# Block-sparse attention and Fourier mixing: gate queries regrouped by key block, the causal bound moved from bias matmuls into the maxima

## The chip, the core and the metric

The kernel runs on one core of a Trainium2 chip. The metric is device time in microseconds of one execution, as the median of several runs. Lower is better. A separate profiled execution gives the profile; its span is the time from the first to the last instruction.

## The reference

There are two stages. The first is attention over 4 batches of 8 heads, 768 positions and 64 features per head. Keys are cut into 12 blocks of 64. A query sees its own block and the three blocks whose mean key scores highest among the blocks that aren't in its future:

```python
k_rep = k.reshape(B, H, n_blocks, block, D).mean(axis=3)
gate_scores = np.einsum('bhsd,bhnd->bhsn', q, k_rep)
gate_scores = np.where(causal, gate_scores, -1000000000.0)
top_idx = np.argsort(gate_scores, axis=-1)[..., -top_k:]
# mask: the chosen blocks and the query's own block, and pos_q >= pos_k
attn = softmax(where(mask, q @ k.T / sqrt(D), -1e9)) @ v
```

The second takes x, the attention output as 4 x 768 x 512, and mixes it with a two-dimensional Fourier transform and a feed-forward layer:

```python
mixed = np.real(np.fft.fft(np.fft.fft(x, axis=1), axis=2))
u = x + mixed
un = (u - mean(u)) / sqrt(var(u) + 1e-6)
out = u + maximum(un @ w_ch1, 0) @ w_ch2        # 512 -> 2048 -> 512
```

## The kernel before

**Units of work.** Two heads of one batch make a pair P, 0 to 15; four pairs make a batch b. For a pair the kernel loads q and k (Lq, Lk: two DMAs each, 192 KB a DMA, three buffers each) and v (Lv, one DMA, two buffers). TensorE transposes both (tq, tk, L306, six 128x128 fp32 blocks each). From the transposed k, DVE sums each block of keys (ks, L311) and spreads the sums for both heads (kh); ACT casts k to fp16 (kc). DVE keeps q in fp32 (qc, L330), GpSimd casts it (qs, through the helper `pcopy` at L242).

**The gate.** g_mm (g) multiplies the fp32 queries by the block sums. Its output has the blocks of one head on 32 partitions and queries along the free axis, in four groups of 32 partitions. For pairs 0 to 6 (P < NX) groups 0 and 1 hold the two halves of the queries from 128 on for one head, groups 2 and 3 those of the other; for pairs 7 to 15 each group holds 192 consecutive queries and both heads. Four more fp16 matmuls (L351, L360) with the tables czl and czr (czl2, czr2) add a huge negative number wherever a block lies in the query's future. g_turn (gt, L366) transposes 32x32 blocks, so that a partition is a query; g_max (gx, L373) takes the eight largest of the 12 values for each query and head, in 10 or 12 instructions; g_less (gl, two steps) marks the blocks that lie below the third largest and multiplies the marks by a table oth (oth2), which is 0 for the query's own block and -60000 elsewhere; g_back (gm, L396) transposes back into the tile mt.

**How the mask reaches the scores.** For pairs 0 to 6 the score tile (s:P,i, L416) gets more matmuls (L427), which add mt for the keys' blocks; SC_MASK lists them. For pairs 7 to 15, stage_K (K, L401) copies mt into rows 64 to 95 of the fp16 q tile, and the scores are one matmul of 96 rows (L421). ACT takes the exponential (e, L436), GpSimd clears the upper triangle of diagonal blocks (d, L442), TensorE multiplies by v (v, L454), DVE divides (x, L465). vc is GpSimd's cast of v.

**The second stage.** fs and fd fold x on DVE, f (f:b,0 to 3, L498 to L508) folds again; y and m are the two Fourier matmuls (L523, L557, L558) with ty (ACT) and tr (DVE, L543) between them; u adds x (L571), xu rescales on ACT, xt and un turn the result into the layout of the feed-forward layer. w:b,it (L633, L635) are the 16 steps of the first feed-forward matmul, r their relu, c (L652) the second matmul, o (L658) the last addition and od the store. bn, nv, nr make the variance. pg:b is a small GpSimd copy that waits for f.

**Weights.** W:0, W:1 (load_w1) and X:0, X:1 (load_w2) are DMAs issued by GpSimd; they cast fp32 to fp16 on the way, 1024 KB each as written. All q, k, v loads and stores are issued by SP. LT brings the Fourier tables, Lc and Li smaller constants.

**The order.** Nothing is scheduled at run time. The text ORDER (L130) is a list of steps such as `g:7` or `s:7,5`, and every engine executes its share of them strictly in this order, with waits on its data and buffers. So moving a step in ORDER moves it in the queue of every engine that it uses. All PSUM tiles come from one pool of four buffers in turn.

Of the kernel before, what the change touches and what calls it, by code (L numbers as in the profile page):

```python
# [19 lines left out]
S = 768  # L20
# [8 lines left out]
def _consts_np():  # L29
# [22 lines left out]
    g, i = p // 32, p % 32  # L52
    b = np.arange(10)
    qq = Q0 + 320 * (g % 2)[:, None] + 32 * b[None, :] + i[:, None]
    oth = np.where((qq // 64)[:, :, None] != nn, NEG, 0.0)

    czl = np.zeros((NB, 32), np.float32)
    czl[:, 0:NB] = np.where(nn[None, :] > nn[:, None], NEG, 0.0)
    czr = 16384.0 * (s[None, Q0:] // 64 == nn[:, None])
# [6 lines left out]
    qq = 192 * (p // 32)[:, None] + 32 * np.arange(6)[None, :] + (p % 32)[:, None]  # L66
    oth2 = np.zeros((128, 6, 2, 16), np.float32)
    oth2[:, :, :, 0:NB] = np.where((qq // 64)[:, :, None, None] != nn, NEG, 0.0)
    czl2 = np.zeros((3, 4, 2, 16), np.float32)
    for gg in range(4):  # L70
        for j in range(3):
            czl2[j, gg, :, 0:NB] = np.where(nn > 3 * gg + j, NEG, 0.0)
    czr2 = 16384.0 * (np.arange(192)[None, :] // 64 == np.arange(3)[:, None])
    ind = np.zeros((2, 32, S), np.float32)
    for e in range(2):
# [7 lines left out]
                czl=czl.astype(np.float16), czr=czr.astype(np.float16),  # L83
                indc=indc.reshape(128, 24).astype(np.float16),
                oth2=oth2.reshape(128, 192).astype(np.float16),
                czl2=czl2.reshape(3, 128).astype(np.float16), czr2=czr2.astype(np.float16),
                ind=ind.transpose(1, 0, 2).copy().astype(np.float16),
                half=half.reshape(128, 24))

# [16 lines left out]
for _pieces in SC_TILES:  # L106
    SC_OFF.append(_w)
    _n = sum(_q1 - _q0 for (_, _q0, _q1) in _pieces)
    _m = []
    _o = 0  # L110
    for (_jt, _q0, _q1) in _pieces:
        for _q in range(_q0, _q1, 128):
            for _e in range(2):
                COL[_e, _jt, _q // 128] = _w + _e * _n + _o + _q - _q0
        for _h in range(2):
            _c0 = Q0 + 320 * _h
            _a = max(_q0, _c0, 192, 128 * _jt + 64)
            _b = min(_q1, _c0 + 320)
            if _a < _b:
                _m.append((_jt, _h, _o + _a - _q0, _a - _c0, _b - _a))  # L120
        _o += _q1 - _q0
    SC_MASK.append(_m)
    _w += 2 * _n
# [7 lines left out]
Lq:1 Lk:1 Lq:2 Lk:2 tk:0 tq:0 ks:0 Lq:3 Lk:3 qc:0 tq:1 iz:1 kh:0 qs:0 g:0 Lq:4 Lv:0 Lv:1 qc:1 iz:0  # L131
kc:0 tk:1 gt:0 gx:0 kc:1 gl:0,0 tq:2 gl:0,1 gm:0 Lq:5 Lk:4 ks:1 s:0,2 s:0,3 qc:2 e:0,2 tk:2 kh:1
e:0,3 Lk:5 g:1 d:0,2 ks:2 qs:1 s:0,4 gt:1 kc:2 qs:2 s:0,0 gx:1 e:0,4 s:0,5 tq:3 kh:2 gl:1,0 e:0,5
Lq:6 s:0,1 qc:3 tk:3 e:0,1 gl:1,1 qs:3 gm:1 g:2 e:0,0 ks:3 d:0,5 tq:4 d:0,4 gt:2 d:0,0 kc:3 s:1,2
kh:3 d:0,1 qc:4 s:1,1 d:0,3 e:1,2 s:1,0 vc:0 gx:2 s:1,3 e:1,1 g:3 Lv:2 Lq:7 gl:2,0 gl:2,1 e:1,3
d:1,1 gm:2 v:0 gt:3 e:1,0 d:1,3 gx:3 s:1,5 s:2,5 x:0 s:2,0 e:1,5 e:2,5 d:1,5 s:2,1 e:2,0 d:2,5
tq:5 gl:3,0 d:1,0 e:2,1 Lq:8 Lk:6 vc:1 s:1,4 qc:5 s:2,4 e:1,4 fs:0,0 s:2,3 Lv:3 fs:0,1 tk:4 gl:3,1
e:2,3 d:1,4 gm:3 tk:5 d:1,2 ks:4 e:2,4 d:2,0 v:1 d:2,1 ks:5 qs:4 kc:4 kh:4 d:2,3 x:1 s:2,2 vc:2
g:4 Lc:0 e:2,2 d:2,4 Lv:4 Lk:7 Lk:8 LT:0 kh:5 qs:5 s:3,2 gt:4 kc:5 s:3,5 gx:4 s:3,0 e:3,5 s:3,1
e:3,2 gl:4,0 tq:6 gl:4,1 e:3,0 d:3,2 gm:4 g:5 d:3,5 qc:6 e:3,1 d:2,2 s:3,4 d:3,0 gt:5 s:4,3 e:3,4  # L140
fs:1,0 s:3,3 gx:5 tq:7 e:3,3 fs:1,1 v:2 gl:5,0 qc:7 d:3,3 d:3,4 gl:5,1 tk:6 vc:3 x:2 e:4,3 s:4,4
d:3,1 Lv:5 ks:6 s:4,0 vc:4 e:4,4 v:3 gm:5 Lv:6 Lq:9 Lk:9 Lq:10 e:4,0 fs:2,1 kh:6 fs:2,0 s:5,5 x:3
kc:6 d:4,0 s:5,1 e:5,5 s:5,0 e:5,1 fd:2,0 s:4,1 fs:3,0 s:5,2 e:5,0 fs:3,1 fd:2,1 g:6 fd:3,0 e:4,1
fd:3,1 s:4,2 gt:6 e:5,2 s:5,4 f:0,3 s:5,3 e:4,2 f:0,2 tk:8 f:0,1 e:5,4 y:0,1 f:0,0 e:5,3 ks:8
d:5,4 d:4,2 y:0,0 tr:0,1 d:5,3 kc:8 W:0 gx:6 d:4,1 s:4,5 d:5,1 ty:0,1 tr:0,0 tk:7 d:5,0 pg:0 d:4,3
e:4,5 ks:7 ty:0,0 m:0,2 W:1 gl:6,0 kc:7 d:5,2 m:0,1 u:0,2 d:5,5 vc:5 m:0,0 u:0,1 xu:0,2 d:4,4 Lv:7
Lk:10 v:5 qs:6 u:0,0 qs:7 xu:0,1 xt:0,2 tq:8 xu:0,0 un:0,2 d:4,5 xt:0,1 kh:8 qc:8 xt:0,0 kh:7
gl:6,1 v:4 qs:8 un:0,1 un:0,0 gm:6 g:7 vc:6 x:5 w:0,1 Lv:8 Lq:11 gt:7 x:4 w:0,3 r:0,1 gx:7 s:6,5
s:6,4 e:6,5 fs:4,1 s:6,2 gl:7,0 e:6,4 w:0,0 fs:5,1 gl:7,1 fs:4,0 e:6,2 gm:7 d:6,4 r:0,3 tq:9 K:7
r:0,0 g:8 Lq:12 Lk:11 qc:9 s:6,1 gt:8 s:6,3 e:6,1 bn:0,3 d:6,2 s:6,0 d:6,5 w:0,7 vc:7 gx:8 e:6,0  # L150
qs:9 e:6,3 tk:9 r:0,7 w:0,8 Lk:12 Lv:9 ks:9 fs:5,0 s:7,5 gl:8,0 r:0,8 w:0,11 kh:9 gl:8,1 kc:9 gm:8
K:8 w:0,2 r:0,11 e:7,5 bn:0,0 s:7,4 r:0,2 g:9 bn:0,1 d:6,3 e:7,4 s:7,0 d:6,0 d:6,1 tq:10 gt:9
e:7,0 bn:0,4 vc:8 s:7,3 qc:10 s:7,1 e:7,3 d:7,0 tk:10 d:7,5 gx:9 d:7,4 e:7,1 s:7,2 Lk:13 Li:0
Lq:13 Lv:10 ks:10 tq:11 e:7,2 d:7,1 w:0,12 gl:9,0 kh:10 kc:10 bn:0,5 d:7,2 X:0 w:0,15 qc:11 r:0,12
gl:9,1 X:1 v:6 r:0,15 bn:0,2 d:7,3 s:8,4 qs:10 gm:9 g:10 e:8,4 x:6 v:7 K:9 gt:10 s:8,5 x:7 s:8,3
e:8,5 w:0,5 e:8,3 gx:10 w:0,10 d:8,3 r:0,5 fs:6,0 fs:6,1 gl:10,0 s:8,2 gl:10,1 r:0,10 fs:7,1
w:0,14 fd:6,1 e:8,2 fs:7,0 fd:6,0 s:8,0 fd:7,1 r:0,14 s:9,5 fd:7,0 w:0,13 e:8,0 f:1,1 f:1,0 e:9,5
s:8,1 r:0,13 s:9,1 qs:11 tk:11 e:8,1 w:0,9 ks:11 e:9,1 vc:9 kc:11 s:9,2 f:1,3 Lv:11 Lk:14 y:1,0
d:8,5 f:1,2 r:0,9 d:8,2 e:9,2 pg:1 s:9,4 vc:10 tr:1,0 tq:12 e:9,4 d:8,4 Lv:12 Lq:14 gm:10 y:1,1
d:8,0 kh:11 ty:1,0 qc:12 d:9,4 vc:11 w:0,6 nv:0 ty:1,1 d:9,2 Lv:13 d:8,1 g:11 tr:1,1 K:10 r:0,6  # L160
tq:13 gt:11 m:1,0 qc:13 s:9,3 u:1,0 s:9,0 e:9,3 w:0,4 gx:11 e:9,0 m:1,1 bn:1,1 r:0,4 d:9,0 d:9,1
s:10,4 xu:1,0 u:1,1 d:9,3 v:8 d:9,5 gl:11,0 un:1,0 s:10,5 gl:11,1 e:10,4 v:9 vc:12 gm:11 bn:1,0
e:10,5 K:11 Lv:14 Lq:15 xu:1,1 x:8 s:10,2 c:0,0,0 e:10,2 un:1,1 fs:8,1 d:10,4 fs:8,0 s:10,3 d:10,2
x:9 s:10,1 vc:13 e:10,3 c:0,1,0 Lv:15 e:10,1 fs:9,1 d:10,3 bn:1,2 nr:0 s:11,5 bn:1,3 s:11,2 e:11,5
s:10,0 s:11,4 e:10,0 c:0,1,1 e:11,4 d:10,1 e:11,2 tk:12 d:11,5 tk:13 Lk:15 ks:12 d:11,2 d:11,4
s:11,3 kh:12 c:0,0,1 ks:13 e:11,3 kh:13 kc:12 d:11,3 qs:13 c:0,4,0 o:0,1 kc:13 od:0,1 o:0,0 d:10,0
# [614 lines left out]
```

## Time and profile before

| | us |
|---|---|
| median of 3 runs | 306.3 |
| lowest and highest | 306.24, 306.63 |
| profiled execution | 307.28 |
| its span | 305.2 |

The costliest groups, as one line each of the page: second feed-forward matmul (L652) 86.0 us busy on TensorE, first one (L633 and L635) 84.7 and 69.7, exponentials (L436) 83.0 on ACT, the diagonal selects (L442) 38.5 on GpSimd.

A row of a group reads: line, engine, operation, output<-input by the program's names, the shape, the count; after the first bar the busy time and the mean duration of one in nanoseconds; after the second bar the engine's idle time just before them and what ended it. DVE, ACT and GpSimd durations can overlap a little in a group, so that busy time by count is nearer to the step from one to the next. Matmuls are pipelined: their durations hold a latency of the pipeline, and the distance from start to start says what a matmul takes of the stream. A timeline's row has start, length, engine, line and, in brackets, idle time before it with its releaser. Rows of a table by stage have the stretch and its length, and then busy time (with the number of instructions) of PE, PEld, DVE, ACT and POOL, TensorE's granted clock, DMA share and GB/s.

### The profile page before, as it was taken

Reading aid. Unit: us, or ns where it says so; the run is one execution under the profiler, and the core shown is the slowest. Engines: PE = TensorE matmul, PEld = TensorE weight load, DVE = VectorE, ACT = ScalarE, POOL = GpSimd, SP = SyncE. Lnnn points to the kernel's source line nnn. Section 1 sums busy time; section 2 is a strip of 40 time slices with the busy share of each in tenths; the row PEclk is TensorE's granted clock in tenths of the full one; section 3 lists DMA queues with packets and bytes.
Section 4 is the critical chain, followed back from the end, with each engine's and each line's share of the span. In section 5 each row is a group of like instructions: output and inputs, shape, how many; then the busy total and the mean of one; then the engine's idle time right before and its main releaser. Section 6 shows DMA issues by size and latency. Waiting matters only on the chain.

```text
span 305.2 us, 6705 instructions
## 1 busy us (share of the span) xinstructions
PE 291.8 (96%) x2638; PEld 179.2 (59%) x2638; DVE 194.4 (64%) x581; ACT 163.2 (53%) x205; POOL 106.5 (35%) x247
## 2 busy tenths in 40 slices
PE   7789996999999999999999999999999999999994
PEld 3557674766676674675577665655666545565441
DVE  1888998999997998699689720773671217700013
ACT  1579989747968967846663779004266001056000
POOL 2165726837682687763470443000030000200000
PEclk9999999999999999999999999999999999999999
DMA  9999989999999998610110001112200011100013
GB/s 172 211 213 206 210 183 274 191 219 193 218 181 194 213 177 163 165 38 34 38 69 2 2 1 34 37 69 71 103 3 0 0 71 69 69 2 0 0 71 137
DMA packets 89467, 32.83 MB, mean 108 GB/s; under 512 B 82704, under 2 KB 85084, under 8 KB 89436
## 3 DMA queue, kind: packets, MB, share of 16 engines
q1 hardware_dynamic: 84108, 27.69, 41.5%
q0 software_dynamic: 3136, 4.19, 8.1%
q10 hardware_dynamic: 2192, 0.52, 0.9%
q8 instruction: 21, 0.34, 0.5%
q14 instruction: 10, 0.08, 0.1%
HBM read 28.73 MB, written 6.29 MB: 115 GB/s over the span
## 4 chain that ended last, share of the span: by engine, by line
PE 80%; DVE 12%; DMA 4%; ACT 2%; SPq 1%; issue 1%; DVEq 0%
PE c L652 27%; PE h L633 18%; PE h L635 9%; PE sc L421 6%; PE av L454 5%; PE tp L306 4%; DMA nat<-in_q_dram 4%; PE yp L523 3%; DVE u L571 2%; PE sc L416 2%; ACT pt L436 1%; PE g L357 1%; PE sc L427 1%; PE mx L557 1%; PE mx L558 1%; DVE tr L543 1%
## 5 line engine op out<-in xcount | busy, mean ns | idle before, releaser
L436 ACT ACTIVATE pt<-sc 128x1024 f16<-128x1024 f32 (+1 forms) x96 | 83.0, 924 | 22.1 <-PE sc L421 15.2
L652 PE MATMUL c<-w_sb,hT 128*128 128x512 f16 x384 | 86.0, 379 | 0.0
L633 PE MATMUL h<-unT,w 128*128 128x512 f16 x256 | 84.7, 379 | 0.0
L635 PE MATMUL h<-unT,w 128*128 128x256 f16 x256 | 69.7, 272 | 0.0
L652 PEld LDWEIGHTS <-hT 128*128 128x128 f16 x384 | 37.3, 98 | 42.7
L645 ACT ACTIVATE hT<-h 128x768 f16<-128x768 f32 x48 | 37.9, 814 | 41.7 <-PE h L635 41.6
L442 POOL TENSOR_SCALAR_AFFINE_SELECT pt<-pt 128x256 f16<-128x256 f16 x96 | 38.5, 422 | 42.3 <-ACT pt L436 41.3
L658 DVE SCALAR_TENSOR_TENSOR u<-c,rs,u 128x512 f32<-128x512 f32 x24 | 17.2, 744 | 46.2 <-PE c L652 46.2
L633 PEld LDWEIGHTS <-w 128*128 128x128 f16 x256 | 25.0, 98 | 28.9 <-issue 0.4
L306 PE MATMUL tp<-id,nat 128*128 128x128 f32 x192 | 26.7, 277 | 3.2 <-DMA nat<-in_q_dram 1.8
L583 ACT ACTIVATE x<-u,nm 128x512 f16<-128x512 f32 x24 | 15.9, 720 | 23.1 <-DVE nm L577 23.0
L242 POOL TENSOR_SCALAR_AFFINE_SELECT qk<-q 64x768 f16<-64x768 f32 (+1 forms) x25 | 20.6, 827 | 18.7 <-DVE q L330 13.1
L635 PEld LDWEIGHTS <-w 128*128 128x128 f16 x256 | 25.0, 98 | 3.5
L421 PE MATMUL sc<-qk 96*128 96x512 f16 (+3 forms) x144 | 26.6, 305 | 0.1
L306 PEld LDWEIGHTS tp<-id,nat 128*128 128x128 f32 x192 | 21.2, 141 | 8.0 <-issue 2.2
L239 POOL TENSOR_TENSOR t<-vr,rs 128x6 f32<-128x6 f32 x12 | 2.5, 207 | 60.5 <-DVE rs L614 59.8
L454 PEld LDWEIGHTS <-pt 128*128 128x128 f16 x672 | 22.1, 97 | 2.3 <-issue 1.0
L454 PE MATMUL av<-v,pt 128*128 128x65 f16 x672 | 23.0, 193 | 0.2
L242 POOL TENSOR_SCALAR_AFFINE_SELECT qk<-mt 32x384 f16<-32x384 f16 x36 | 18.6, 518 | 10.0 <-DVE mt L396 8.4
L643 DVE TENSOR_SCALAR hT<-h 128x768 f16<-128x768 f32 x16 | 15.0, 945 | 10.3 <-PE h L635 10.3
L571 DVE SCALAR_TENSOR_TENSOR u<-mx,x 128x512 f32<-128x512 f32 x24 | 15.5, 684 | 8.7 <-DMA out_dram<-u 4.4
L537 ACT CAST ty<-yp 128x772 f16<-128x772 f32 x8 | 8.0, 1045 | 19.2 <-PE yp L523 18.0
(84 smaller groups left out, 357.9 us busy)
## 6 DMA issues: line engine op xcount, KB each, us to landing
nat<-in_v_dram SPq DMA_DIRECT2D x16, 384.0 KB, 6.0
out_dram<-u SPq DMA_DIRECT2D x24, 256.0 KB, 2.0
nat<-in_k_dram SPq DMA_DIRECT2D x31, 192.0 KB, 4.5
nat<-in_q_dram SPq DMA_DIRECT2D x31, 192.0 KB, 5.1
w<-in_moe_w_ch_dram POOLq DMA_DIRECT2D x2, 1024.0 KB, 11.2
w_sb<-in_moe_w_ch_dram POOLq DMA_DIRECT2D x2, 1024.0 KB, 14.1
fs_sb<-c_FS SPq DMA_DIRECT2D x1, 582.0 KB
fd_sb<-c_FD SPq DMA_DIRECT2D x1, 384.0 KB, 6.4
```

Of the source, the lines that this page charges most:

```text
L242: nc.gpsimd.affine_select(out=out, in_=in_, pattern=[[0, i] for i in n], base=0, channel_multiplier=0, compare_op=ALU.is_ge, fill=0.0)
L306: nc.tensor.transpose(ps[:, 128 * st:128 * st + 128], src[:, st, :], id32)
L421: nc.tensor.matmul(ps[:, e, co:co + q1 - q0], qk[0:96, e, 1, 128 * jt:128 * jt + 128], qk[0:96, e, 0, q0:q1], start=True, stop=True)
L436: nc.scalar.activation(out=d["pt"][:, o:o + 2 * n].rearrange("p (e c) -> p e c", e=2), in_=d["sc", i][:, :, 0:n], func=AF.Exp, scale=0.125)
L442: nc.gpsimd.affine_select(out=dg, in_=dg, pattern=[[0, 2], [1, 128]], base=0, channel_multiplier=-1, compare_op=ALU.is_ge, fill=0.0)
L454: nc.tensor.matmul(av[:, e, 66 * st:66 * st + 65], pt[:, co:co + 128], vv[:, e, jt, 0:65], start=(cnt == 0), stop=(cnt == 20))
L571: nc.vector.scalar_tensor_tensor(out=u_b[:, k2, :].rearrange("p (m two) -> p two m", two=2), in0=mps[:, k2, :].rearrange("p (two m) -> p t ...
L633: nc.tensor.matmul(hp[:, 0:512], w1s, unT[:, dt, 0:512], start=(dt == 0), stop=(dt == NDT - 1))
L635: nc.tensor.matmul(hp[:, 512:768], w1s, unT[:, dt, 512:768], start=(dt == 0), stop=(dt == NDT - 1))
L645: nc.scalar.activation(out=hT, in_=hp, func=AF.Relu)
L652: nc.tensor.matmul(c_ps[b, g[0]][:, st - g[0], :], h_t[b, it][:, 128 * st:128 * (st + 1)], w2_sb[:, it, :], start=(it == 0), stop=(it == N ...
L658: nc.vector.scalar_tensor_tensor(out=o, in0=c_ps[b, g[0]][:, st - g[0], :], scalar=st_t[b][1][:, st:st + 1], in1=o, op0=ALU.mult, op1=ALU.add)
```

## The change

Queries of a gate are regrouped, so that all rows of a column block have the same own key block. For pairs 0 to 6 a group takes every other run of 32 queries; for pairs 7 to 15 every fourth run. Blocks of 64 queries thus lie side by side in different groups, and the number of blocks that a query may see depends, nearly everywhere, on the column block alone. g_max can then take its maximum over just the allowed blocks (at least eight values), and no bias matmul is needed. Where fewer than eight blocks are allowed, the values beyond the bound are overwritten: by a minimum with a table lim for pairs 0 to 6, by three memsets for pairs 7 to 15. Column blocks whose queries see three or fewer blocks are left out. The table oth is now the same for all rows. The mask's matmuls and stage_K's copies follow the new grouping: each is split in two.

The core of the diff (tables of constants, and the tiles' declarations, cut):

```diff
 def g_mm(P):            # pairs 0 to 6
+            qq = d["q32"][:, Q0:S].rearrange("p (b w i) -> p b w i", w=2, i=32)
             for c in range(4):
-                c0 = Q0 + 320 * (c % 2)
-                nc.tensor.matmul(g[32 * c:32 * c + 32, :], kr_s[slot][:, c // 2, :],
-                                 d["q32"][:, c0:c0 + 320], start=True, stop=False)
-            for c in range(4):
-                c0 = 320 * (c % 2)
-                nc.tensor.matmul(g[32 * c:32 * c + 32, :], czl, czr[:, c0:c0 + 320],
-                                 start=False, stop=True)
+                nc.tensor.matmul(g[32 * c:32 * c + 32, :].rearrange("p (b i) -> p b i", i=32),
+                                 kr_s[slot][:, c // 2, :], qq[:, :, c % 2, :], start=True, stop=True)
...
 def g_turn(P):
+        if P < NX:
+            d["gt"] = gt = apool.tile([128, 320], FP, tag="gt", name=f"gt_{P}", bufs=1)
+            nc.vector.transpose(out=gt, in_=d["g"])
+            x = gt.rearrange("p (b n) -> p b n", n=32)[:, 1:5, 4:8]
+            tt(x, x, lim, ALU.min)
+            return
...
+        nc.vector.memset(gt[0:64, 35:205].rearrange("p (b c) -> p b c", c=34)[:, :, 0:17:16], -3e38)
+        nc.vector.memset(x[:, 1, :, 4:6], -3e38)
+        nc.vector.memset(x[:, 1:3, :, 6:8], -3e38)
 def g_max(P):
-        for j in range(nj):
-            nc.vector.max(out=mx[:, j, :], in_=d["gt"][:, w * j:w * j + NB])
+        for j in range(1 if P < NX else 2, nj):
+            n = max(8, j + 3 if P < NX else j // 2 * 2 + 2)
+            nc.vector.max(out=mx[:, j, :], in_=d["gt"][:, w * j:w * j + n])
 def g_less(P, j):       # pairs 7 to 15: ten column blocks of 12 in place of 12 of 16
-            tt(d["lt"], d["lt"], oth2, ALU.mult)
+                tt(l, l, oth2.rearrange("p b e n -> p (b e) n")[:, 2:12, 0:NB], ALU.mult)
...
 def stage_K(P):
         for c in range(4):
-            pcopy(qk_s[P % NSLOT][64:96, :, 0, 192 * c:192 * c + 192],
-                  mt[32 * c:32 * c + 32, :].rearrange("p (o x) -> p o x", o=1)
-                  .to_broadcast([32, 2, 192]), [2, 192])
+            for e in range(2):
+                pcopy(qk_s[P % NSLOT][64:96, e, 0, :]
+                      .rearrange("p (b w i) -> p b w i", w=4, i=32)[:, :, c, :],
+                      mt[32 * c:32 * c + 32, :].rearrange("p (b i) -> p b i", i=32), [6, 32])
 def s_mm(P, i):         # pairs 0 to 6: the mask
-        for jt, w, o, a, wid in (SC_MASK[i] if P < NX else []):
-            for e in range(2):
-                nc.tensor.matmul(ps[:, e, o:o + wid], indz[w][hs[e], 128 * jt:128 * jt + 128],
-                                 mt[hs[e], a:a + wid], start=False, stop=True,
-                                 skip_group_check=True)
+        for jt, o0, o1, a in (SC_MASK[i] if P < NX else []):
+            for w in range(2):
+                for e in range(2):
+                    nc.tensor.matmul(ps[:, e, o0:o1].rearrange("p (b w i) -> p b w i", w=2, i=32)
+                                     [:, :, w, :], indz[w][hs[e], 128 * jt:128 * jt + 128],
+                                     mt[hs[e], a:a + (o1 - o0) // 2].rearrange("p (b i) -> p b i", i=32),
+                                     start=False, stop=True, skip_group_check=True)
```

The memsets and loads of the four bias tables go; a load of lim (8 KB) and a memset of the now permanent tile ltb come.

ORDER is written anew from the first step to the last. It holds the same steps, each once. Two excerpts show its manner; first the loads and the beginning, then the surroundings of the first feed-forward step `w:0,1`:

```diff
-Lq:1 Lk:1 Lq:2 Lk:2 tk:0 tq:0 ks:0 Lq:3 Lk:3 qc:0 tq:1 iz:1 kh:0 qs:0 g:0 Lq:4 Lv:0 Lv:1 qc:1 iz:0
+Lk:1 Lk:2 Lq:1 Lq:2 tk:0 tq:0 ks:0 Lq:3 Lk:3 qc:0 tk:1 iz:1 kh:0 qs:0 g:0 ks:1 iz:0 gt:0 kc:0 tk:2
...
-gl:6,1 v:4 qs:8 un:0,1 un:0,0 gm:6 g:7 vc:6 x:5 w:0,1 Lv:8 Lq:11 gt:7 x:4 w:0,3 r:0,1 gx:7 s:6,5
+vc:5 kc:8 ks:7 v:4 d:5,5 u:0,1 W:1 xu:0,0 m:0,2 d:5,2 d:5,3 ks:8 X:0 s:6,3 xu:0,1 u:0,2 v:5 e:6,3
+kh:7 x:4 s:6,5 xu:0,2 d:6,3 s:6,2 qs:7 x:5 xt:0,1 e:6,5 e:6,2 s:6,1 un:0,1 xt:0,2 d:6,5 e:6,1 qs:8
+xt:0,0 un:0,2 g:7 un:0,0 s:6,0 s:6,4 gt:7 e:6,0 d:6,1 tq:9 fs:5,1 Li:0 Lv:7 gx:7 e:6,4 w:0,1 Lq:12
+d:6,0 kh:8 bn:0,4 d:6,4 tk:9 gl:7,0 r:0,1 gl:7,1 w:0,7 gm:7 kc:9 qc:9 K:7 w:0,0 r:0,7 ks:9 w:0,2
```

Further steps that stand elsewhere in it: before, W:0 stood behind tr:0,1, d:5,3 and kc:8 and ahead of pg:0; now it stands behind pg:0, vc:4, d:4,2 and d:4,3. Before, X:0 and X:1 stood near pair 7's and 8's scores; now X:0 follows W:1 and X:1 stands near pair 8's scores. y:0,0 now stands between f:0,0 and f:0,3. Before, Lq:9 and Lk:9 stood behind Lv:6; now Lq:9, Lk:8, Lv:5, Lq:10 and Lk:9 stand ahead of Lv:6.

## The prediction

> **What bounds the kernel now.** I read the page's busy shares and slices first, then the same by stage, then the chain of waits in order of time, then the groups kept apart by shape, then DMA and timelines of single stretches.
>
> ```profile
> PE 291.8 (96%) x2638; PEld 179.2 (59%) x2638; DVE 194.4 (64%) x581; ACT 163.2 (53%) x205; POOL 106.5 (35%) x247
> ...
> 0.00:9.00 9.00, 6.60 (x25) 3.16 (x26) 2.20 (x7) 1.49 (x2) 1.90 (x18) 1.00 0.92 172
> 9.00:41.00 32.00, 29.25 (x434) 20.18 (x434) 28.77 (x111) 26.42 (x33) 16.23 (x32) 1.00 1.09 205
> 41.00:66.00 25.00, 21.07 (x319) 15.39 (x318) 23.35 (x63) 19.70 (x25) 14.29 (x25) 1.00 1.09 223
> 66.00:118.00 52.00, 51.87 (x551) 35.24 (x548) 47.71 (x158) 40.95 (x52) 33.28 (x62) 1.00 1.06 195
> 118.00:301.00 183.00, 183.00 (x1318) 105.28 (x1316) 91.61 (x244) 74.67 (x95) 40.77 (x112) 1.00 0.16 45
> ```
>
> Columns: stretch, length, busy PE, PEld, DVE, ACT, POOL, granted clock, DMA share, GB/s. From 66 us, the first step w of the feed-forward, TensorE never stands still: what leaves its stream there comes off the end. Before 66 us DVE is the fullest (28.8 of 32, 23.4 of 25), DMA is full too. Busy PE flatters: a 512-column c matmul takes 1.73 / 8 = 0.216 us of stream (chain), 0.42 ns a column. Starts against columns leave PE gaps of 7.5 us from 9 to 41, about 8.2 from 41 to 66, 3.5 from 66 to 118 (2.0 in gaps over 60 ns), 5.3 after.
>
> ```profile
> 49.80 1.02 DVE L239 TENSOR_TENSOR fg<-zw 128x762 f16<-128x762 f16 x2
> ...
> 53.23 1.02 DVE L543 CAST tr<-yp 128x768 f16<-128x768 f32 x1 [1.26 <-PE yp L523]
> 54.14 0.80 DVE L373 MAX8 mx<-gt 128x8 f32<-128x12 f32 x10
> 55.15 1.03 DVE L543 CAST tr<-yp 128x768 f16<-128x768 f32 x1 [0.20 <-PE yp L523]
> ```
>
> So even in batch 0's Fourier stage DVE waits only 1.5 us for y.
>
> ```profile
> L373 DVE MAX8 mx<-gt 128x8 f32<-128x12 f32 x178 | 14.3, 155 | 0.2
> L242 POOL TENSOR_SCALAR_AFFINE_SELECT qk<-mt 32x384 f16<-32x384 f16 x36 | 18.6, 518 | 10.0 <-DVE mt L396 8.4
> L360 PE MATMUL g<-czr,czl 128*32 128x192 f16 x36 | 2.4, 246 | 0.0
> L351 PE MATMUL g<-czr,czl 128*32 128x320 f16 x28 | 2.2, 299 | 0.0
> ...
> 71.73 0.53 PE L357 MATMUL g<-q,krb 128*32 128x192 f32 x8
> 72.08 0.27 PE L360 MATMUL g<-czr,czl 128*32 128x192 f16 x4
> 72.28 0.39 PE L416 MATMUL sc<-qk 64*128 64x256 f16 x4
> ```
>
> The four bias matmuls of a gate run side by side in four column groups: one pass, not four. Last view, DMA from 54 to 64 us, while the casting load of w1 runs on POOL's queue q0 and all q, k, v loads stand on q1:
>
> ```profile
> q0 software_dynamic: 881, 1.77, 96.0%
> q1 hardware_dynamic: 711, 0.18, 13.0%
> ```
>
> **What the Trainium skill says.** "TensorEngine Tiling (Array Packing)", Key Properties: changing the tiling mode drains TensorE. The trace agrees: from the first bias matmul to the score matmul behind it 0.20 us pass, 0.08 of them columns. That drain stays. "PSUM — Partial Sum Buffer", Specifications: non-contiguous access patterns slow matmuls significantly; no matmul of before writes PSUM with gaps, so this trace can't say. "DMA: Bandwidth & Descriptors", Issuing engines are not separate DMA queues: SP's and POOL's transfers share 16 engines and interleave. The trace shows how unevenly: 1.77 MB against 0.18.
>
> **The change, part by part.** The profiled execution took 307.28 us, 305.2 of span and 2.1 around it; the runs' median is 306.3. I sum differences and put them on 306.3.
>
> *Bias matmuls gone.* 7 gates lose 320 columns (0.135 us each, 0.95), 9 lose 192 (0.081, 0.73). The nine lie in or near the full stretch: -0.7. The seven lie where PE has gaps: worth 0 to -0.9; I take 0. The gate's query is now read in runs of 32 fp32 at a stride: no row; 0 to +0.3 us a gate (its fp32 passes doubled, 0.32); I take 0, since runs are long.
>
> *Mask matmuls (pairs 0 to 6).* 11 two-head couples become 16 of half width; columns stay 2176 a head and pair (0.91 us of stream, both heads side by side). The 64-wide ones were already issued 29 ns apart, so only the two 32-wide ones cost more than columns: 7 x 0.03 = 0.2 us in the stage with gaps, 0. Gapped PSUM writes: below, as a rival.
>
> *DVE.* Pairs 0 to 6: one MAX less (14.3 / 178 = 0.08), one small tensor_tensor more (the 128x24 one takes 0.17 to 0.21; I take 0.17), shorter compares -0.03: +0.06 x 7 = +0.4. Pairs 7 to 15: two MAX less (-0.16), 72 elements less in compare and product (-0.13), three memsets more (the 128x6 one takes 0.063): -0.1 x 9. Near zero; the limit of extent saves at most 4 ns a MAX.
>
> *POOL.* stage_K goes from 4 copies of 384 elements to 8 of 192. From 422 ns at 256, 518 at 384 and 826 at 768 elements a 192 one costs about 0.374: 3.0 us in place of 2.07, +8.3 over nine pairs. POOL is busy 35%, so only latency counts. For pair 7 the new order has two w and one gate between gm and the first score (2 x 1.28 + 0.47 = 3.0 us of PE), where before 5.6 us stood: 0 to 1.5 (if a copy stays at 0.5); I take +0.5.
>
> *Constants.* Four small tables go, one (8 KB) comes; ACT's queue issues one DMA less and SP two less. All behind the first loads: 0.
>
> *The order.* ORDER is rewritten throughout with the same steps, so each engine's queue moves. I compared which steps stand ahead of three points. Ahead of the first w: newly all six score tiles of pair 6 and tq:9 (PE +2.7 us), x:4, fs:5,1, gt:7, gx:7 (DVE +2.7 net of kh:8). DVE sets that point, so w starts 2.7 + 0.4 later; y:0,0 is now begun while f:0,3 and f:0,2 still run on DVE, and qc:8 and gl fill its wait, which takes back up to 1.5 us of waiting: w starts 1.6 later, with 2.7 of PE work less behind it: -1.1. From there to the first c: c:0,0,0 comes ahead of 7.8 us of DVE and 5.3 of PE steps, so PE gets filler that needs no DVE; of the 2.0 us in larger gaps (0 to -2.0) I take -0.6. After 118 us nothing is to be had: the last tail (c, o, od) has the same form.
>
> *SP and POOL queues.* SP brings the q and k loads in another order. To the start of W:0's packets (53.4 us) q1 had moved 11.1 MB, in written order up to Lv:6. X:0 stood near 86 us; now W:0, W:1 and X:0 follow one another on POOL. At 6.4 us each (1.77 MB in 10 us, 1.05 MB each; X nearer 7) they take the engines for about 20 us, not 13. W:0 itself comes later: f ends about 1 us later, and pg:0, vc:4 and two selects (0.18 + 0.90 + 2 x 0.42) stand ahead: packets from about 56.2, with 11.1 + 2.8 x 0.21 = 11.7 MB moved. The load that PE wants first behind this is Lk:9, complete at 11.9 MB, wanted by tk:9 near 69 us (behind the first w). The missing 0.2 MB come at 18 KB/us x 13 us = 0.23 MB: just in time. I take 0.
>
> Sum: -0.7 - 1.1 - 0.6 + 0.5 = -1.9: 304.4 us.
>
> **Rivals.**
> *A, the forecast:* 304.4, own range 302.8 to 305.6.
> *B, only what is certain:* the new order's gains are paid back by small stalls of its own; then the bias passes' 0.7 less the wait for K: 306.1. For: each order is laid by estimates. Against: PE has filler ahead of each DVE group.
> *C, slower: the third weight load starves Lk:9.* If under about 11.65 MB are moved when W:0's packets begin, the trickle doesn't finish it, and tk:9, which stands in PE's queue ahead of w:0,7, waits to near 75.5 us. Price up to 6.5 us: 304.4 + 6 = 310; a late half costs 2 to 3. For: the margin above is a few hundred kB. Against: q1 stood below its rate from 40 to 45 us before (slices 183 after 210) and may gain.
> *D, slower: gapped PSUM writes.* If the mask matmuls take twice their columns, 7 x 0.91 = 6.4 us come into the stage with 15.7 us of PE gaps; about half hidden, 304.4 + 3.2 = 307.6. Twice is an estimate from the page's "significantly"; runs of 32 columns speak for less, a gain is excluded.
>
> **How the numbers follow.** A 0.45, better than A's range 0.03, B 0.13, C 0.23, D 0.12, other stalls of the order 0.04. A difference under 0.2% (0.6 us) can't be told from none here. Faster 0.48, same 0.13 (B), slower 0.39. The range 302.6 to 309.0 leaves out the best 0.03 and the worse half of C, and takes in D and the unknown strides; A's own stands above.
>
> **What would show it.** Right: no bias group; a gate followed by its successor after 0.47 us; first w near 67.5 us with pair 6's scores ahead; PE gaps from 66 to 118 under 3 us; PE full after. K copies near 0.37 us. Wrong: a gap ahead of tk:9 ended by a k load (C); L427's 128-wide and 64-wide starts further apart than their columns (D); gate starts further apart than 0.16 us; first pair-7 score late by more than 1.5 us on POOL's copies.

## The result and the profile after

| | before | after |
|---|---|---|
| median, us | 306.27 | 315.40 |
| lowest and highest | 306.12, 306.63 | 313.85, 316.50 |
| profiled execution, its span | 307.28, 305.2 | 315.76, 313.8 |

The change makes the kernel slower: 1.0293 of the time before, 95% interval 1.0247 to 1.0339. Forecast were 304.4 us, range 302.6 to 309.0. (Of some versions below, single executions take several us longer than the others: the medians count them, the ratios leave the longest out.)

The page of after, its slices (each digit tenths of a slice of 7.8 us; PEclk is the granted clock) and the chain of waits:

```profile
PE   7798999873999999999999999999999999998995
...
PEclk9999999996899999999999999999999999999999
...
PE 80%; DMA 10%; DVE 4%; SPq 3%; issue 1%; ACT 0%; POOL 0%; DVEq 0%
```

Two slices of PE, from 63 to 78 us, fall to 7 and 3 tenths, and from 71 to 86 us the granted clock falls as well. Nothing else in the row stands out. So the loss sits in one place. TensorE's waits of after, the longest first (total, times, longest):

```profile
PE tp L291 <- DMA nat<-in_k_dram: 8.6, 3, 7.4
...
PE c L648 <- ACT hT L641: 0.9, 1, 0.9
...
PE tp L291 <- DVE u L567: 0.8, 1, 0.8
```

In before's list of TensorE's waits no load of k stands at all. The place, in TensorE's timeline of after:

```profile
68.08 0.38 PE L629 MATMUL h<-unT,w 128*128 128x512 f16 x1
68.30 0.27 PE L631 MATMUL h<-unT,w 128*128 128x256 f16 x1
75.95 1.51 PE L291 MATMUL tp<-id,nat 128*128 128x128 f32 x6 [7.38 <-DMA nat<-in_k_dram]
77.26 0.63 PE L629 MATMUL h<-unT,w 128*128 128x512 f16 x1
77.68 0.42 PE L631 MATMUL h<-unT,w 128*128 128x256 f16 x1
...
80.40 0.38 PE L629 MATMUL h<-unT,w 128*128 128x512 f16 x1
80.62 0.27 PE L631 MATMUL h<-unT,w 128*128 128x256 f16 x1
```

w:0,1 ends, and tk:9 waits for Lk:9. Then everything takes longer until 80.4 us: from one L629 to the next L631 0.42 us pass instead of 0.22. The table by stage says why. Its columns are those of the prediction's first view; the number after POOL's is the granted clock:

```profile
66.00:68.40 2.40, 2.40 (x22) 1.49 (x16) 2.30 (x19) 1.94 (x2) 1.39 (x4) 1.00 1.15 198
68.40:73.50 5.10, 0.17 (x2) 0.00 (x0) 1.78 (x5) 0.81 (x1) 3.86 (x11) 1.00 1.22 197
73.50:80.30 6.80, 4.35 (x16) 2.65 (x17) 0.24 (x1) 1.59 (x2) 1.05 (x2) 0.50 1.05 218
```

TensorE stands from 68.4 us; at 73.5 its clock is halved, for 6.83 us in the records, to 80.33. From 75.95 on TensorE works 4.4 us at half clock and loses 2.2.

I laid the whole difference out over TensorE's stream: the starts of its instructions against the columns that they have (0.42 ns each; these sums depend a little on how matmuls that run side by side are counted, by up to 0.2 us a row). Before ends at 300.88 us = 271.38 of columns + 29.50 of gaps; after at 309.76 = 269.68 + 40.08. Half speed counts as gap here.

| us | before | after | difference |
|---|---|---|---|
| columns | 271.38 | 269.68 | -1.70 |
| gaps 0 to 66 | 20.73 | 20.04 | -0.69 |
| 66 to 80 | 0.82 | 9.67 | +8.85 |
| 80 to 118 | 2.68 | 2.50 | -0.18 |
| 118 to 145 | 1.13 | 2.15 | +1.02 |
| 145 to 200 | 2.25 | 2.51 | +0.26 |
| from 200 | 1.89 | 3.21 | +1.32 |

So 8.85 us come from the stall and the half clock behind it, and two small new gaps add 1.0 (ahead of tk:13, which waits for a PSUM tile that u:1,2 reads) and 1.07 (in the last tail). Up to 118 us there are gains as forecast, -1.70, -0.69 and -0.18; which of them shorten the kernel is taken up at the end.

Last, the transfers of after from 55 to 75 us, with the casting weight loads on q0 and the q, k, v loads on q1 (packets, MB, share of 16 engines):

```profile
q0 software_dynamic: 2089, 3.14, 87.3%
q1 hardware_dynamic: 3714, 0.93, 28.1%
```

Three weight loads, 3.14 MB, go through in 20 us, while the q, k and v loads get 0.93 MB. Lk:9's halves were issued at 54.24 and 55.99 us and landed at 73.35 and 75.81.

### The profile page after: what moved, and what is told of

The parts are those of the page before. It is cut to its first block, busy times and chain, and to the rows that moved or that the text cites. A ratio compares the mean times of both kernels' runs of the same rounds, so it can differ in the third digit from the quotient of the medians.

```text
span 313.8 us, 6743 instructions
## 1 busy us (share of the span) xinstructions
PE 292.7 (93%) x2644; PEld 179.1 (57%) x2644; DVE 193.5 (62%) x591; ACT 163.6 (52%) x205; POOL 110.9 (35%) x279
## 4 chain that ended last, share of the span: by engine, by line
PE 80%; DMA 10%; DVE 4%; SPq 3%; issue 1%; ACT 0%; POOL 0%; DVEq 0%
PE c L648 27%; PE h L629 18%; PE h L631 9%; DMA nat<-in_k_dram 8%; PE sc L415 7%; PE av L450 6%; PE tp L291 5%; PE yp L519 3%; SPq L274 2%; DMA nat<-in_v_dram 2%; PE mx L553 1%; PE mx L554 1%; PE g L341 1%; PE sc L410 1%; PE yp L525 1%
## 5 line engine op out<-in xcount | busy, mean ns | idle before, releaser
L629 PE MATMUL h<-unT,w 128*128 128x512 f16 x256 | 86.2, 384 | 0.0
L631 PE MATMUL h<-unT,w 128*128 128x256 f16 x256 | 70.4, 275 | 0.0
L438 POOL TENSOR_SCALAR_AFFINE_SELECT pt<-pt 128x256 f16<-128x256 f16 x96 | 37.6, 411 | 50.0 <-ACT pt L432 49.1
L629 PEld LDWEIGHTS <-w 128*128 128x128 f16 x256 | 25.3, 99 | 29.2 <-issue 1.7
L291 PE MATMUL tp<-id,nat 128*128 128x128 f32 x192 | 27.6, 282 | 11.4 <-DMA nat<-in_k_dram 8.6
L229 POOL TENSOR_SCALAR_AFFINE_SELECT qk<-mt 32x192 f16<-32x192 f16 x72 | 25.4, 373 | 10.1 <-DVE mt L389 8.5
L631 PEld LDWEIGHTS <-w 128*128 128x128 f16 x256 | 25.3, 99 | 4.0
L226 POOL TENSOR_TENSOR t<-vr,rs 128x6 f32<-128x6 f32 x12 | 2.4, 198 | 56.8 <-DVE rs L610 56.2
L310 ACT CAST qk<-tp 64x768 f16<-64x768 f32 x18 | 14.3, 792 | 8.5 <-PE tp L291 8.4
```

Of the source, the lines that this page charges most:

```text
L229: nc.gpsimd.affine_select(out=out, in_=in_, pattern=[[0, i] for i in n], base=0, channel_multiplier=0, compare_op=ALU.is_ge, fill=0.0)
L291: nc.tensor.transpose(ps[:, 128 * st:128 * st + 128], src[:, st, :], id32)
L438: nc.gpsimd.affine_select(out=dg, in_=dg, pattern=[[0, 2], [1, 128]], base=0, channel_multiplier=-1, compare_op=ALU.is_ge, fill=0.0)
L629: nc.tensor.matmul(hp[:, 0:512], w1s, unT[:, dt, 0:512], start=(dt == 0), stop=(dt == NDT - 1))
L631: nc.tensor.matmul(hp[:, 512:768], w1s, unT[:, dt, 512:768], start=(dt == 0), stop=(dt == NDT - 1))
```

## The experiments

Theory T: Lk:9 is caught behind three weight loads in a row on POOL's queue, which get nearly all of the DMA engines; the stall and the half clock after it are the loss. Rivals: R1, the new gate itself costs time; R2, the new order loses in other places. The first four runs shared one chip; before there was 306.81 us (305.59 to 308.65).

### X:0 moved away

```diff
- ... d:5,3 ks:8 X:0 s:6,3 xu:0,1 ...        + ... d:5,3 ks:8 s:6,3 xu:0,1 ...
- ... Lk:11 d:7,3 K:8 g:9                    + ... Lk:11 d:7,3 K:8 X:0 g:9
```

> The changed kernel with one step moved: X:0 (the third weight load) from behind W:1 to behind K:8. Theory T (the q and k loads stand still while three weight loads run one behind the other; tk:9 waits for Lk:9, and TensorE then runs at half clock for a while): the stall of 7.5 us and the 2.2 us lost at half clock go, 315.4 - 9.7 = 305.7, between 304.7 and 307. Rival R1 (the new gate itself costs: more GpSimd copies, gapped PSUM writes, more small DVE work): stays at 312 or more. Rival R2 (the rewritten order loses in many places): 309 to 313.

Measured: median 309.95 us (307.06 to 315.85), ratio 1.0083 (1.0041 to 1.0124). Two of the seven executions took 307.1 and 307.3, four 309.5 to 310.9; the profiled one was the longest, 315.85. In its trace the stall behind the first w is gone, but another load was caught, Lk:8's second half, issued 1.4 us before W:0 (in after 4.0 us before it):

```profile
62.89 1.51 PE L291 MATMUL tp<-id,nat 128*128 128x128 f32 x6 [4.55 <-DMA nat<-in_k_dram]
```

The expected 304.7 to 307 was missed by all seven, by 0.3 us or less in the two shortest. X:0 does make the loss larger: the median fell by 5.4 us. In the profiled execution the load that was caught had been issued 2.9 us later than in after, and when W:0's packets began 10.59 MB had moved, in place of 11.26 in after. What the four of 309.5 to 310.9 lost, no trace shows.

### Lk:9 ahead of Lq:10

```diff
- ... d:3,1 Lv:5 Lq:10 Lk:9                  + ... d:3,1 Lv:5 Lk:9 Lq:10
```

> The changed kernel with two neighbouring loads exchanged: Lk:9 is issued ahead of Lq:10; the three weight loads stay together. T: Lk:9 needs 11.5 MB moved in place of 11.9, lacks about 0.25 MB when the weight loads begin and comes with the trickle near 62 to 64 us, ahead of its use at 68.4; Lq:10 comes near 75.8 and is wanted near 78. So 305.5 to 307.5. If the weight block as such harms (POOL, HBM traffic), not the order of the loads: 312 or more. R1: 312 or more.

Measured: 306.39 us (305.73 to 311.76), ratio 0.9991 (0.9974 to 1.0009). Two tokens exchanged bring back 9 us, with all three weight loads where they were. Gaps from 66 to 80 us are 0.78 us; TensorE's waits on k loads fall from 8.6 to the first line below (its list of waits), and the clock row of the page has no dip:

```profile
PE tp L291 <- DMA nat<-in_k_dram: 1.0, 2, 0.6
```

```profile
PEclk9999999999999999999999999999999999999999
```

T holds: the caught load is the loss. The margin is small: Lk:9's second half landed at 66.85 us, about 1.5 us ahead of its use.

### The new gate in the old order, and the old gate in the new order

The first takes all functions of after and ORDER of before, the second the reverse.

> The new gate with the order of the kernel before. T: the gate is no cost; TensorE loses 1.7 us of stream, of which 0.7 in the full stretch: 305.0 to 306.5. R1: most of the 9 us appears, 311 or more. In between (307 to 310) would say that the longer copies of stage_K cost where the old order leaves little room.

Measured: 306.78 us (305.54 to 309.03), ratio 1.0002 (0.9980 to 1.0024). R1 falls. Nor does the gate gain anything that could be measured: columns fall by about 1.6 us, but gaps grow by 0.89 before 66 us and by 0.32 from 80 to 118.

> The kernel before with the new order: old gate with bias matmuls. T: the same wait ahead of tk:9 and the same half clock, 315 to 318 (1 us above the changed kernel at most, for the bias matmuls). R1: near 306 to 309.

Measured: 316.85 us (315.37 to 318.64), ratio 1.0335 (1.0292 to 1.0378). The old gate in the new order shows the same picture, with a longer wait at the same transposes and the same 6.83 us of half clock. Its tk:9, in TensorE's timeline:

```profile
77.11 1.51 PE L306 MATMUL tp<-id,nat 128*128 128x128 f32 x6 [8.30 <-DMA nat<-in_k_dram]
```

The order alone carries the loss, and the run with Lk:9 first says which two of its steps. So R2 falls as well, but for the two small gaps.

### The stall filled with idle work

```diff
 def a_tp(P, who):
+        for _ in range(32 if (P, who) == (9, 1) else 0):
+            nc.tensor.matmul(ps[:, 0:512], id16, fs_sb.rearrange("p a b c k -> p (a b c k)")[:, 0:512],
+                             start=True, stop=True)
```

> The kernel after, and ahead of tk:9's six transposes 32 matmuls of 512 columns that nobody reads, into the same PSUM tile (32 x 0.213 = 6.8 us, so from 68.4 to 75.2 us of the stall's 75.9). Theory T (the half clock behind the stall is the answer to an idle TensorE and a cost of its own, 4.4 us at half = 2.2 us): the load still lands at about 75.8 us, the transposes still start at about 75.9, but no stretch of granted clock 0.5 follows, and the time is 315.4 - 2.2 = 213.2 us plus 100, that is 313.2 (312.3 to 314). Rival (the half clock has another cause than the idle engine, as the transfers or the chip): the stretch at half clock stays and the time is 315.4 or, with the matmuls themselves slowed to half, more.

Measured: 313.15 us (312.23 to 313.44), ratio 1.0196 (1.0159 to 1.0233); 2.25 us less than after in the medians, 3.0 us less by the ratios to before, with nothing else changed. (This run, the next two and the one that moves u:1,2 shared a chip, with before at 306.95.) TensorE's timeline (the added matmuls, then tk:9), and the row by stage for the stretch that was at half clock:

```profile
67.75 7.07 PE L291 MATMUL tp<-fs_sb,id 128*128 128x512 f16 x32
74.66 0.82 PE L295 MATMUL tp<-id,nat 128*128 128x128 f32 x6
75.31 0.38 PE L633 MATMUL h<-unT,w 128*128 128x512 f16 x1
```

```profile
73.50:80.30 6.80, 6.80 (x50) 3.99 (x48) 3.17 (x6) 3.29 (x5) 0.47 (x1) 1.00 0.93 193
```

The six transposes take 0.82 us instead of 1.51, the clock stays at 1.00. So the half clock is the answer to the idle engine and a bill of its own, beside the wait: about 2.2 us here. (In this one execution Lk:9 landed 1.6 us earlier, at 74.17, the first w came 0.7 us earlier and tk:9 waited 0.6 us less; the 2.25 rests on the medians.)

### The last tail

On top of Lk:9 ahead of Lq:10, in w:3,... and r:3,... the numbers 0 and 8 and the numbers 7 and 15 change places, so that the last ReLU is one of the second half:

```diff
- w:3,9 r:3,5 w:3,7 r:3,9 w:3,0 r:3,7 r:3,0 c:3,2,0
+ w:3,9 r:3,5 w:3,15 r:3,9 w:3,8 r:3,15 r:3,8 c:3,2,0
```

> The kernel after with Lk:9 ahead of Lq:10, as in the run of that name, and the last batch's first-layer steps relabelled (0 with 8, 7 with 15, places kept), so that the last one belongs to the second half of the second layer. Theory (the gap of 1.07 us ahead of the first second-layer matmul of the last batch comes only from which half the last ReLU belongs to): the gap goes, and 306.4 becomes 305.3 (304.8 to 305.8). Rival (the gap moves to the first matmul of the second half, or the load decides again): 306.4.

Measured: 305.34 us (304.62 to 312.67), ratio 0.9939 (0.9916 to 0.9963), as the theory had it. The group of the second layer's matmuls, in before, in after and here; the last column is TensorE's wait ahead of them:

```profile
L652 PE MATMUL c<-w_sb,hT 128*128 128x512 f16 x384 | 86.0, 379 | 0.0
```

```profile
L648 PE MATMUL c<-w_sb,hT 128*128 128x512 f16 x384 | 86.2, 379 | 0.9 <-ACT hT L641 0.9
```

```profile
L648 PE MATMUL c<-w_sb,hT 128*128 128x512 f16 x384 | 86.2, 379 | 0.0
```

c:3,2,0 reads the ReLUs 0 to 7. In after the last w is w:3,0, so c waits for its ReLU on ACT; before it was one of the second half, and the first half's c covered it.

### X:0 third in a row in the kernel before

```diff
- ... ty:0,0 m:0,2 W:1 gl:6,0 ...            + ... ty:0,0 m:0,2 W:1 X:0 gl:6,0 ...
- ... d:7,2 X:0 w:0,15 ...                   + ... d:7,2 w:0,15 ...
```

> The kernel before, whole, with one load moved: X:0 from its place at about 83 us to directly behind W:1, so that three weight loads stand in a row as in the kernel after. In before Lq:9 lands at 66.5 and 67.9 us, as W:1 ends at 67.1, and tq:9 wants it at 71.0. Theory T (what follows in a row behind W:0 decides, and not the rest of the order): Lq:9, Lk:9 and Lq:10 land only as the third load ends, at about 74 to 75 us; tq:9 waits 3 to 4 us, a stretch at half clock may follow, and the time is 309 to 312.5 us. Rival (the rest of the order, which asks for other tiles at other times, is what makes the row harmful): 306.3, with no gap ahead of tq:9.

Measured: 313.67 us (311.61 to 314.63), ratio 1.0201 (1.0159 to 1.0243): slower, as T has it, but above its range. The places were only half foreseen. TensorE's waits:

```profile
PE sc L421 <- DMA qk<-c_ind: 3.3, 1, 3.3
PE tp L306 <- DMA nat<-in_k_dram: 2.9, 3, 1.9
```

Lq:9 came at 68.3 us and wasn't waited for; tk:9 waited 1.9 us for Lk:9. The longer wait lies 20 us later: all of SP's loads had slipped by about 5 us, so that a table of 96 KB for slot 0, issued at 85.2 us before, now went out at 90.4, behind X:1 (88.3), and landed 10.4 us later instead of 3.9. One load moved on POOL's queue makes two loads late, one of them on the far side of the next weight load. So the row of three harms this order too. The profiled execution is the shortest of the four and has no half clock; two of the others have a mean granted clock of 0.987 and 0.988, as after has with its 6.83 us (0.987), so a stretch of half clock is likely there, though no trace of them shows it.

### W:0 later, in the kernel after

```diff
- tk:7 W:0 gm:6 ... vc:5 kc:8 ...            + tk:7 gm:6 ... vc:5 W:0 kc:8 ...
```

> The kernel after, whole, with Lk:9 still behind Lq:10 and X:0 still third, but W:0 moved on GpSimd's queue behind vc:5, that is from 52.7 to about 56.0 us: its first packets at about 58.0 us instead of 54.8. Theory T (what decides is how much of the loads has moved before W:0's packets begin, 11.9 MB for all of Lk:9, of which 11.25 had moved in after): 3.2 us at 0.2 MB per us bring 11.9 MB, Lk:9 lands at about 58 to 60 us or, if it is just missed, its second half still late; with Lk:9 in time 306.4 (305.5 to 308, with a wait of the first w of up to 1 us in it). Rival (three weight loads in a row in themselves, or the rest of the order, make the stall, wherever they start): 313 to 317, the stall only moved.

Measured: 307.92 us (307.26 to 309.36), ratio 1.0045 (1.0029 to 1.0060), on a chip with before at 306.59. W:0's packets began at 58.89 us, with 12.26 MB moved by the other queues (after: 54.76 us and 11.26 MB). Lk:9's halves landed at 58.07 and 58.97, and from 66 to 80 us TensorE's gaps are 0.78. So 7.5 us of the 9 are back with Lk:9 still last and three weight loads still in a row. It is the amount that has moved at W:0's start that decides, and it is a cliff: 4.1 us later at the start, 17 us earlier at the end. The remaining 1.5 us over the Lk:9-first run go with a gap that wasn't expected, 2.0 us at 53.6; the last three runs are about it.

### The two gaps left, and the margin

Moving the sum u:1,2 away from the store it waits for (on top of the relabelled tail):

```diff
- s:10,5 m:1,2 gm:12 ... c:0,2,1 u:1,2 e:11,4 ... tk:13 e:10,3 d:10,5 d:11,3
+ s:10,5 gm:12 ... c:0,2,1 e:11,4 ... tk:13 m:1,2 e:10,3 d:10,5 u:1,2 d:11,3
```

> As the run before it but one (Lk:9 first, last batch relabelled), and in batch 1 the mixing step m:1,2 and its sum u:1,2 moved back by about eight steps of the order, behind tk:13: in the traces u:1,2 waits 2.9 us for a store of u to leave, and tk:13 waits 1.0 us for the PSUM tile that u:1,2 reads. Theory (the gap of 1.2 us at 129 us comes from that store alone): the gap goes and 305.3 becomes 304.2 (303.7 to 304.9). Rival (the wait only moves to another tile): 305.3.

Measured: 305.05 us (304.23 to 313.26), ratio 0.9934 (0.9917 to 0.9951), not to be told from the 0.9939 without it. The trace (of a long execution) has the rival's picture: the wait for u:1,2 now lies ahead of a score tile, 0.8 us in place of 0.9.

Three of its 21 executions took 307.3 to 313.3 us. The profiled one was among them (309.74), and in it Lk:9's halves landed at 64.3 and 71.5: caught again, and followed by half clock, 3.41 us of it:

```profile
71.58 1.51 PE L291 MATMUL tp<-id,nat 128*128 128x128 f32 x6 [3.59 <-DMA nat<-in_k_dram]
```

When W:0's packets began, 11.24 MB had moved here, and 11.27 in the Lk:9-first run, where the load still came in time: that order stands close to the same cliff. So in the order of the tail run W:0 was moved:

```diff
- tk:7 W:0 gm:6 ... m:0,1 d:5,4              + tk:7 gm:6 ... m:0,1 d:5,4 W:0
```

> The kernel of the run with Lk:9 first and the last batch relabelled, and W:0 moved on GpSimd's queue behind five of its diagonal masks (d:5,4), which lets it start 1.9 us later. Theory (the single runs of 309 to 313 us among those of 305.3 are runs in which a small delay of the loads lets W:0 catch one of them; 1.9 us are about 0.38 MB of margin at 0.2 MB per us): the median stays at 305.3 (304.7 to 306), and no run, or one, lies above 307. Rivals: the scatter has another cause, and a tenth of the runs still lies above 307; or W:0 comes too late for the first w at 67.1 us (it landed at 63.0 to 63.5, so 1.9 later is 65.4) and the median rises by up to 1 us.

Measured: 306.55 us (306.13 to 307.76), ratio 1.0003 (0.9988 to 1.0018). No execution is several us longer than the others, but the median rose by 1.2 (by the ratios 2.0), and six of 14 lie above 307, where at most one was expected. TensorE's list of waits has none of the first w. Again TensorE stands 2.0 us at 53.6. GpSimd's and VectorE's timelines of this run:

```profile
51.15 0.89 POOL L229 TENSOR_SCALAR_AFFINE_SELECT v<-nat 128x768 f16<-128x768 f32 x1
52.01 2.55 POOL L438 TENSOR_SCALAR_AFFINE_SELECT pt<-pt 128x256 f16<-128x256 f16 x7
54.51 0.95 POOL L703 DMA_DIRECT2D w<-in_moe_w_ch_dram  x1
```

```profile
51.07 0.95 DVE L315 COPY q<-tp 128x768 f32<-128x768 f32 x1
51.94 2.69 DVE L226 TENSOR_TENSOR lt<-lt,oth 128x108 f16<-128x108 f16 x1
54.55 1.00 DVE L539 CAST tr<-yp 128x768 f16<-128x768 f32 x1
```

A product of 108 elements, 0.216 us in the median of its seven, takes 2.69 us: to the end of seven masks in a row on GpSimd. In the order with the earlier W:0 it took 0.89, to the end of the two masks ahead of W:0. The Trainium skill, "SBUF — State Buffer", SBUF: two separate sides, says that VectorE and GpSimd share a pair of ports as an exclusive lock, and that an operation of VectorE with two SBUF inputs needs it against a GpSimd operation that reads SBUF; the loser waits for the whole instruction. The product has two SBUF inputs. So it was moved ahead of the masks:

```diff
- gl:6,0 y:0,1 pg:0 qc:8 vc:4 ty:0,0 gl:6,1   + gl:6,0 gl:6,1 y:0,1 pg:0 qc:8 vc:4 ty:0,0
```

> The kernel of the run with the later W:0 and Lk:9 first, and in gate 6 the mask product on VectorE (gl:6,1, two SBUF inputs) moved from behind a copy to directly behind the comparison gl:6,0. In the run before it this product took 2.69 us (median 0.22), from the start to the end of seven diagonal masks that GpSimd ran back to back (52.01 to 54.56), and TensorE stood 2.0 us at 53.6 us for what VectorE does next. Theory L (VectorE waits while GpSimd holds what both read SBUF through; W:0 used to interrupt the seven masks after the second): moved ahead of them the product takes at most 0.9 us (one cast of v), the gap at 53.6 us goes, and the median is 305.3 (304.7 to 305.9) with no run above 307. Rival (another reason for the gap, as the load of the next tile or ScalarE's order): the gap and 306.5 stay.

Measured: 308.01 us (306.95 to 309.42), ratio 1.0025 (1.0009 to 1.0041); a miss, and it settled the point:

```profile
51.16 3.44 DVE L226 TENSOR_TENSOR lt<-lt,oth 128x108 f16<-128x108 f16 x1
54.52 0.94 DVE L315 COPY q<-tp 128x768 f32<-128x768 f32 x1
```

It now began 0.04 us behind GpSimd's cast of v and was held through the cast and all seven masks, 0.89 + 2.55 us, where I had allowed for one instruction. The gap grew to 2.75 us. So the product was given to GpSimd itself, for pair 6 alone, in the order of the run with W:0 behind d:5,4:

```diff
-                tt(l, l, oth[:, 1:10], ALU.mult)
+                tt(l, l, oth[:, 1:10], ALU.mult, nc.gpsimd if P == 6 else None)
```

> The kernel with Lk:9 first, the last batch relabelled and the later W:0 (the order of the run before the last, the mask product gl:6,1 in its first place), and this one product of gate 6 made by GpSimd itself instead of VectorE. The run before showed that the product held up VectorE for 3.44 us, through a cast and seven masks that GpSimd ran in a row, and not for one of its instructions. Theory L (VectorE waits for the whole unbroken row of GpSimd's instructions, so that only an operation of two SBUF inputs is to be kept out of it): with no such operation on VectorE between 51 and 54.6 us the stop goes, the gap of 2.0 to 2.8 us at 53 us goes, and the time is that of the order with the earlier W:0, 305.3 (304.7 to 306), with no run above 307. Rival (VectorE's other operations are held too, or the product on GpSimd is late for the transposition): 306.5.

Measured: 305.52 us (304.41 to 307.84), ratio 0.9954 (0.9938 to 0.9969), with before at 306.63. GpSimd's timeline, and VectorE's next operation, which no longer waits for it:

```profile
51.95 0.37 POOL L226 TENSOR_TENSOR lt<-lt,oth 128x108 f16<-128x108 f16 x1
52.28 2.55 POOL L438 TENSOR_SCALAR_AFFINE_SELECT pt<-pt 128x256 f16<-128x256 f16 x7
```

```profile
52.46 1.04 DVE L539 CAST tr<-yp 128x768 f16<-128x768 f32 x1 [0.51 <-ACT ty L533]
```

The gap is gone: between 51 and 54.6 us VectorE copies, casts and transposes beside the same cast of v and seven masks, and only the operation with two SBUF inputs had been held. Of its 22 executions one lies above 307 us, of the two versions with the relabelled tail and the earlier W:0 four of 29: too few to show that the margin did it.

Three versions of the changed kernel thus take 0.5 to 0.7% less than before: the relabelled tail (0.9939), the same with u:1,2 moved (0.9934) and the last one (0.9954). Their intervals overlap.

## Why the prediction was wrong

**The step that failed** stands under "SP and POOL queues": "packets from about 56.2, with 11.1 + 2.8 x 0.21 = 11.7 MB moved ... The missing 0.2 MB come at 18 KB/us x 13 us = 0.23 MB: just in time. I take 0." W:0's packets began at 54.76 us, with 11.26 MB moved; 0.64 MB were missing, not 0.2. (11.1 and 11.26 both count q10's 0.52 MB; q1 alone had moved 10.6 and 10.74.) The delay that I gave W:0 (2.8 us, worked out from steps ahead of it) was 1.34. GpSimd's timelines up to W:0, in before and in after, show why:

```profile
50.49 1.30 POOL L442 TENSOR_SCALAR_AFFINE_SELECT pt<-pt 128x256 f16<-128x256 f16 x3 [2.98 <-ACT pt L436]
51.74 0.96 POOL L713 DMA_DIRECT2D w<-in_moe_w_ch_dram  x1
```

```profile
50.98 0.23 POOL L507 COPY gone<-fg 1x4 f16<-1x4 f16 x1 [5.83 <-DVE fg L226]
52.73 0.95 POOL L703 DMA_DIRECT2D w<-in_moe_w_ch_dram  x1
```

In before W:0 stood behind three selects that waited for exponentials; that wait is gone in after, and the forecast put the new steps on top of it. And f ended at 51.1 us in before and at 51.0 in after, not 1 us later. The new steps took 1.75 us from there (1.92 forecast), W:0 was issued 1.0 us later than in before, and its packets followed 0.35 us more slowly. Of the 0.44 MB between 11.7 and 11.26, this error of 1.46 us is 0.31 at 0.21 MB per us; the other 0.13 is a lower rate of the loads before W:0.

The trickle (what the q, k and v loads get beside the weight loads) was better than taken, 0.39 MB from 55 to 65 us, and still too little: at 68.4 us, where tk:9 stands, 11.77 MB had moved, and 11.9 only at 72.0. The length of the three weight loads was right, 20.8 us for about 20 (though 1.05 MB at 1.77 MB in 10 us is 5.9 us a load, not the 6.4 written there). The runs with Lk:9 first and with W:0 later confirm the account in two ways: 0.4 MB less to wait for, or 1.0 MB more moved, and the stall is gone.

A margin of nothing was read as a cost of nothing. The step named the right load, the right waiter and the right cliff, and then took the one value at which it costs nothing: 0.03 MB to spare, where W:0's start alone was off by 0.31.

**Rival C** had the mechanism, with a chance of 0.23, and priced it at up to 6.5 us. It was 7.54 us of stall on TensorE's stream (7.38 in the records), and then 2.2 us at half clock, which the prediction didn't have. The Trainium skill could have told: "TensorE: Matmul & The Clock Gate", The HAM clock gate, has TensorE fall to half rate after an idle window of about 3.4 us. This trace agrees: idle from 68.4 us, half from 73.5, for 6.83 us, twice 3.41; the long execution with u:1,2 moved had one such stretch, 3.41 us. A stall of this length has to be priced with its cold restart.

**The last tail.** "After 118 us nothing is to be had: the last tail (c, o, od) has the same form" was wrong by 1.07 us: the steps have the same form, but the last ReLU belongs to the other half (the tail run). The new 1.0 us at u:1,2 wasn't looked for either.

**What held.** *Bias matmuls:* columns -1.70 against 0.95 + 0.73. But the new gate alone gave 1.0002 (0.9980 to 1.0024), so the -0.7 taken for the nine is at the edge of what that run allows. *First w:* at 67.11 us, 67.5 forecast. *Gaps from 66 to 118:* without the stall 3.0 us in the Lk:9-first run against 3.5 before, close to the -0.6. Together these two terms were -1.7; from the gate in the old order to the new order without stall and tail gap (1.0002 to 0.9939) it is -1.9 us. *K:* the row

```profile
69.53 2.95 POOL L229 TENSOR_SCALAR_AFFINE_SELECT qk<-mt 32x192 f16<-32x192 f16 x8 [1.02 <-DVE mt L389]
```

shows pair 7's eight copies in 2.95 us (3.0 forecast), 0.373 each (0.374). The +0.5 for them appears nowhere: in the Lk:9-first run no score tile waits for them. *D:* refuted. The 160-column mask matmuls with gapped outputs start 65 ns apart, and 160 columns at 0.42 ns are 67; all of these matmuls are busy 13.6 us (224 of them) against 13.3 before (154).

Put on the 306.3 us of before, the best orders take 0.9934 to 0.9954 of it, 304.3 to 304.9. So A's size was met by an order without the caught load and the tail gap; the wrong sign came from C. That the sum fits is in part luck: the -0.7 for the bias matmuls doesn't show in the gate-alone run, nor the +0.5 for K's copies in the new order.

## What to carry to other kernels

Where a DMA burst of one queue starves another, work out how many bytes must have moved before it starts, put errors on both numbers, and price the step on both sides of the cliff instead of taking its edge; then issue the load that is wanted first ahead of the burst, whatever its neighbours. The TensorE stall of 7.5 us was billed twice here: filling it with dead matmuls gave back 2.25 us, and a stall of 3.6 us was still followed by half clock. And a step that issues a DMA on an engine's queue can be what parts a long row of that engine's work, so moving it can make another engine wait.

## What the runs showed that was not expected

- VectorE's product of two SBUF inputs was held through a whole unbroken row of GpSimd's instructions: 0.89, 2.69 and 3.44 us for the same 0.216 us, as GpSimd had two masks, seven masks, or a cast and seven masks in a row. The skill's page has the lock for the length of one instruction; here it wasn't given up between eight, and the measurement decides. With W:0's DMA issue behind the second mask the product ended there (0.89 us); copies, casts and transpositions of VectorE ran beside the same cast and masks.
- The halving of the clock came 5.1 us after TensorE went idle, lasted 6.83 us and ran on for 4.4 us after work had resumed. In the long execution with u:1,2 moved a shorter stall was enough: idle from 67.8 to 71.6 us, half clock from 71.3, for 3.41 us. The wait of 3.3 us in the run with X:0 third in before brought none.
- Casting loads on GpSimd's queue took 1.66 MB in the 10 us from 55 us on, where the q, k and v loads got 0.39 MB; by themselves these moved 1.72 MB in the 9.7 us before.
